# Second product accumulated onto the first, a quarter moved to GpSimd, the last rows in one transfer: attention and a mixture of experts on one core

## The chip, the core and the metric

The kernel runs on one core of a Trainium2 chip. The metric is the time of one execution on the device in microseconds; a number for a kernel is the median of its runs. The engines are TensorE (PE, with its weight loader PEld), VectorE (DVE), ScalarE (ACT), GpSimd (POOL) and SyncE (SP), which only issues transfers here. Transfers run on 16 DMA engines that the queues of SP and ACT share.

## The reference

Rotary attention over 2 batches x 8 heads x 576 positions x 64, then a dense mixture of 4 experts over the 1152 rows of 512 that come out of it.

```python
def rotate(x):
    x1, x2 = (x[..., :half], x[..., half:])
    return np.concatenate([x1 * cos - x2 * sin, x1 * sin + x2 * cos], axis=-1)
scores = scale * np.matmul(q_rot, k_rot.transpose(0, 1, 3, 2))
attn = softmax(scores)                      # over the keys, with 1e-9 in the divisor
x = np.matmul(attn, v)                      # as 1152 rows of 512
p = domain_probs / (domain_probs.sum(-1, keepdims=True) + 1e-09)
for e in range(4):
    h = np.maximum(x @ w1[e], 0.0)          # 512 -> 1024
    out += p[:, e:e + 1] * (h @ w2[e])      # 1024 -> 512
```

## The kernel before

All matrices of the experts are split into a high and a low part (`wh`, `wl`, `xH`, `xL`, `hH`, `hL`), and a product is three matmuls: high by high, high by low, low by high. `split` writes the high part on one engine (for weights ACT, L136) and the low part on another (for weights POOL, L143).

The rows go through the experts in two chunks: chunk 0 is 512 rows of batch 0, interleaved with the attention of batch 1; chunk 1 is the other 640 rows and starts at about 349 us, with nothing else running beside it. Its 640 rows end in `acc1_0` to `acc1_4`, of 128 rows each; `acc1_4` holds the last 64 rows of both batches, which lie 576 rows apart in the output.

Chunk 1 (`Moe1`) makes the first layer `x @ w1` with seven products of quarter size in place of eight (a Strassen-Winograd scheme). `TERMS` names for each of `p1` to `p7` a weight operand (a quarter of `w1` or a sum `s0` to `s3` of quarters) and a row operand (a quarter of `x`, or a sum `t1` to `t4`). The sums of weights are made by `Weights.sum`: four additions into `sf` (L538; on DVE, for the very first block on POOL), then `split` into `sh` (ACT) and `sl` (POOL). The sums of rows are made by `Quarters`: `whole` joins high and low (L666), `less` subtracts (L671), `high` and `low` split again (`tH`, L678 on ACT; `tL`, L682). They are issued in steps spread over the end of chunk 0; the last five steps come just before chunk 1, with the sums `s2`, `s3` of the second half on DVE.

A product is six matmuls of 128 x 320 (two j by three parts) into one of eight PSUM banks, which `bank` hands out in turn: four for `p1` of the four blocks of the first expert, four (`ahead`) for `p2`, then round. What follows a product is written in `product`: ACT copies `p1` to SBUF; DVE adds `p1` to `p6` (giving `u`), `u` to `p7` (`v`), and so on; `hidden` adds a remaining term in PSUM on DVE (L789), lets ACT write the high half of the hidden row through Relu (L797) and leaves the low half on DVE (L799) for after the next product. In the first expert the order is `p1` of the four blocks, `p2` of the four blocks, then `p6 p7 p5 p4 p3` per block; in the others `p1 p6 p7 p5 p2 p4 p3` per block.

The second layer (`second_layer`) is 8 x 5 x 3 matmuls of 128 x 512 into five banks `po`, each followed after its last matmul by `mix` on DVE (L633), which adds the weighted result to `acc`. In the last expert `mix` also stores: four times 128 rows from the SP queue (L639), and for `acc1_4` two halves of 64 rows, one from SP and one from ACT (L642).

`wts.next()` loads the next block of weights (SP) and splits an earlier one (ACT, POOL, and for `w1` DVE too). `second_layer` calls it four times per expert, `first_layer` after `p4` of each block. Every engine works in the order in which the program issues to it; waits are set by the framework from what reads and writes which tile.

Of the kernel before, what the change touches and what calls it, by code (L numbers as in the profile page):

```python
# [56 lines left out]
def kernel(  # L57
# [17 lines left out]
    nc = tc.nc  # L75
# [6 lines left out]
    SM = NR * P  # L82
# [398 lines left out]
    class Weights:  # L481
# [47 lines left out]
        def sum(self, raw, e, fb):  # L529

            a = raw.rearrange("p (j k h f) -> p j k h f", j=2, h=2, f=P)
            a11, a12, a21, a22 = (a[:, j, :, h, :] for h in range(2) for j in range(2))
            x = self.pool.tile([P, 4, 2, P], F32, tag="sf", name=f"sf{e}_{fb}", bufs=2)
            for o, p, q, op in (
                (0, a21, a22, ALU.add), (2, a11, a21, ALU.subtract), (1, x[:, 0], a11, ALU.subtract),
                (3, a12, x[:, 1], ALU.subtract),
            ):
                (nc.vector if e or fb else nc.gpsimd).tensor_tensor(out=x[:, o], in0=p, in1=q, op=op)  # L538
            sh, sl = (
                self.pool.tile([P, 4, 2, P], F32R, tag=f"s{t}", name=f"s{t}{e}_{fb}", bufs=NF // FB) for t in "hl"  # L540
            )
            split(nc.scalar, nc.gpsimd, x, sh, sl)
            self.sums[e, fb] = sh, sl

        def next(self):
# [3 lines left out]
    class Moe:  # L549
# [77 lines left out]
        def mix(self, e, t, po):  # L627
# [8 lines left out]
            if e == E - 1:  # L636
# [3 lines left out]
                else:  # L640
                    for b in range(B):
                        (nc.sync, nc.scalar)[b].dma_start(  # L642
                            out=out[b * S + SM : (b + 1) * S, :], in_=acc[b * ST : (b + 1) * ST]
                        )

    class Quarters:
# [46 lines left out]

        def second(self, eng, j):

# [6 lines left out]
            yield True  # L702
            self.whole(eng, "s3", j, 1, 0)
            self.less(eng, "s3", ("s3", "s2"))
            self.low(eng, "s0", 2, j)
# [15 lines left out]
    class Moe1(Moe):  # L721
# [7 lines left out]
        def __init__(self, ctx, quarters):  # L729
# [6 lines left out]
            ]  # L736
            self.used, self.ahead = 4, [self.bank(f"p2_{i}", i) for i in range(4)]
            self.x, self.lows = {}, []
# [9 lines left out]
        def product(self, e, i, p):  # L748
# [7 lines left out]
            (wh, wl), (xh, xl) = ws, self.quarters.operand(x)  # L756
            o = self.bank(f"{p}{e}_{i}")[:, 0:TH]
            for j in range(2):
                nc.tensor.matmul(o, lhsT=wh[:, j], rhs=xh[:, j], start=(j == 0), stop=False)  # L759
                nc.tensor.matmul(o, lhsT=wh[:, j], rhs=xl[:, j], start=False, stop=False)  # L760
                nc.tensor.matmul(o, lhsT=wl[:, j], rhs=xh[:, j], start=False, stop=(j == 1))  # L761
            x, lows = self.x, self.lows
            self.lows = []
            if p == "p1":
                x["p1", i] = self.temp("p1", e, i, NF // FB)
                nc.scalar.activation(out=x["p1", i], in_=o, func=AF.Copy)
# [9 lines left out]
            elif p == "p2":  # L776
                self.hidden(e, 2 * i, 0, o, x["p1", i])
            elif p == "p4":
# [11 lines left out]

        def hidden(self, e, f, t, o, other):

            if f not in self.hh:
                self.hh[f] = [self.h.tile([P, self.n], F32R, tag=f"h{x}{f}", name=f"h{x}1_{e}_{f}") for x in "HL"]
            hi, lo = (x[:, t * TH : (t + 1) * TH] for x in self.hh[f])
            self.add(o, o, other)
            nc.scalar.activation(out=hi, in_=o, func=AF.Relu)  # L797
# [6 lines left out]
        def first_layer(self, e):  # L804
# [3 lines left out]
            if e == 0:  # L808
                for i in range(nb):
                    self.product(e, i, "p1")  # L810
                wts.next()
                for i in range(nb):
# [4 lines left out]
            for i in range(nb):  # L817
                for p in ("p6", "p7", "p5", "p4", "p3") if e == 0 else ("p1", "p6", "p7", "p5", "p2", "p4", "p3"):
                    self.product(e, i, p)
                    if p == "p4" and e:  # L820
                        wts.next()
# [14 lines left out]
        def second_layer(self, e):  # L836
            n = self.n
            po = [self.bank(f"po1_{e}_{t}") for t in range(n // P)]
            for f in range(NF):
                fb, fi = divmod(f, FB)  # L840
                wH, wL = (w[:, fi, :] for w in wts.got[1, e, 1, fb])
                for t in range(n // P):
# [4 lines left out]
                    if f == NF - 1:  # L847
                        self.mix(e, t, po[t])
                if fi == FB - 1:
                    wts.next()  # L850
# [296 lines left out]
```

## Time and profile before

| what | us |
|---|---|
| runs (3): median, lowest, highest | 568.88, 568.68, 569.23 |
| the profiled execution | 566.62 |
| its span, first to last instruction | 564.8 |
| PE busy | 539.7 (96%) |
| POOL busy | 339.3 (60%) |
| DVE busy | 324.0 (57%) |
| ACT busy | 281.0 (50%) |

All views below are of the one profiled execution, and their times count from the first instruction. In a row of a timeline the first number is the start, the second the duration; in brackets stand the idle time of the engine before it and the instruction that ended it. A matmul's duration is longer than its step: they overlap in the array, so idle time is read from starts or from the brackets. The granted TensorE clock is 0.996 of full speed (2.4 GHz) over the span, and 1.00 wherever PE works from 349 us on.

### The profile page before, as it was taken

To read this page: it belongs to the slowest core of one execution; us is meant where nothing else is said; L and a number is where in the kernel's file an instruction comes from. 1 tells how busy PE (TensorE), PEld (TensorE's weight loads), DVE (VectorE), ACT (ScalarE), POOL (GpSimd) and SP (SyncE) were. 2 spreads that over 40 slices of the span, in tenths; PEclk is the share of its full clock that TensorE was granted. 3 is DMA by queue.
4 is the path that set the end of the run, shared out by engine and by line. 5 is a ranking of instruction groups with operands and counts; after the bars stand their busy time and mean duration, and the time that the engine had idled before them with its cause. 6 is when DMAs were issued, how large, how long until landed. Compare 5 with 4: busy or idle time off the path is not lost. (4 is left out here: it accounts for less than half of the span.)

```text
span 564.8 us, 8507 instructions
## 1 busy us (share of the span) xinstructions
PE 539.7 (96%) x3157; PEld 474.3 (84%) x3157; DVE 324.0 (57%) x587; ACT 281.0 (50%) x561; POOL 339.3 (60%) x240
## 2 busy tenths in 40 slices
PE   4898998999999999999999999999999999999996
PEld 3787887788888888888888888888898899889985
DVE  5588897244363534453344546994587668757702
ACT  5688888555444545555545553453344234324400
POOL 7999984558715871487433487458554655565400
PEclk9899999999999999999999999999999999999999
DMA  5245023352234123432142214522223213222102
GB/s 153 71 117 145 17 51 99 81 173 93 77 113 140 41 76 102 131 97 64 62 128 74 62 52 150 185 76 74 77 77 111 74 39 113 78 76 85 61 1 93
DMA packets 48732, 50.68 MB, mean 90 GB/s; under 512 B 15538, under 2 KB 38322, under 8 KB 48690
## 3 DMA queue, kind: packets, MB, share of 16 engines
q1 hardware_dynamic: 47890, 49.38, 29.0%
q10 hardware_dynamic: 800, 0.75, 0.5%
q8 instruction: 25, 0.41, 0.3%
q14 instruction: 17, 0.14, 0.1%
HBM read 43.34 MB, written 2.36 MB: 81 GB/s over the span
## 5 line engine op out<-in xcount | busy, mean ns | idle before, releaser
L143 POOL TENSOR_TENSOR wl<-wr,wh 128x1024 fp32r<-128x1024 f32 x64 | 154.4, 2413 | 136.0 <-ACT wh L136 136.0
L136 ACT ACTIVATE wh<-wr 128x1024 fp32r<-128x1024 f32 x64 | 67.2, 1052 | 26.5 <-PE po L600 11.9
L300 DVE TENSOR_REDUCE mx<-sc 128x1 f32<-128x576 f32 x72 | 54.2, 753 | 37.7 <-PE sc L289 37.0
L143 POOL TENSOR_TENSOR sl<-sf,sh 128x1024 fp32r<-128x1024 f32 x16 | 38.5, 2407 | 43.0 <-ACT sh L136 43.0
L846 PE MATMUL po<-wh,hL 128*128 128x512 f32 x160 | 62.3, 389 | 0.0
L845 PE MATMUL po<-wl,hH 128*128 128x512 f32 x160 | 62.3, 389 | 0.0
L844 PE MATMUL po<-wh,hH 128*128 128x512 f32 x160 | 62.3, 389 | 0.0
L308 ACT ACTIVATE e<-sc,mx 128x576 f32<-128x576 f32 x72 | 53.3, 740 | 17.7 <-DVE mx L300 16.7
L584 DVE SCALAR_TENSOR_TENSOR hL<-ph,hH 128x512 fp32r<-128x512 f32 x32 | 22.1, 692 | 60.1 <-ACT hH L583 60.1
L598 PE MATMUL po<-wh,hH 128*128 128x512 f32 x128 | 52.3, 409 | 0.0
L136 ACT ACTIVATE sh<-sf 128x1024 fp32r<-128x1024 f32 x16 | 17.0, 1060 | 70.5 <-DVE sf L538 64.9
L623 PE MATMUL ph<-xH,wh 128*128 128x512 f32 x128 | 51.5, 402 | 0.0
L624 PE MATMUL ph<-xL,wh 128*128 128x512 f32 x128 | 50.1, 392 | 0.4 <-POOL xL L424 0.4
L343 DVE TENSOR_TENSOR ptL<-pp,ptH 128x512 fp32r<-128x512 f32 x64 | 44.0, 687 | 11.1 <-ACT ptH L339 10.3
L339 ACT ACTIVATE ptH<-pp 128x512 fp32r<-128x512 f32 x64 | 38.1, 595 | 24.6 <-PE x L372 17.3
L600 PE MATMUL po<-wh,hL 128*128 128x512 f32 x128 | 50.3, 393 | 0.0
L625 PE MATMUL ph<-xH,wl 128*128 128x512 f32 x128 | 50.1, 392 | 0.0
L599 PE MATMUL po<-wl,hH 128*128 128x512 f32 x128 | 50.0, 391 | 0.0
L797 ACT ACTIVATE hH<-p 128x320 fp32r<-128x320 f32 x64 | 27.1, 436 | 40.3 <-DVE p L789 40.3
L322 PE MATMUL pp<-ident,e 128*128 128x128 f32 x288 | 44.7, 279 | 2.1 <-DVE ptL L343 1.1
L538 DVE TENSOR_TENSOR sf<-wr 128x256 f32<-128x256 f32 x30 | 32.7, 1129 | 16.9 <-DMA wr<-in_moe_w_dram 16.9
L322 PEld LDWEIGHTS pp<-ident,e 128*128 128x128 f32 x288 | 34.2, 142 | 8.1 <-ACT e L308 2.4
(171 smaller groups left out, 1373.4 us busy)
## 6 DMA issues: line engine op xcount, KB each, us to landing
wr<-in_moe_w_dram SPq DMA_DIRECT2D x68, 512.0 KB, 3.6
k2T<-kT SPq DMA_DIRECT2D x14, 288.0 KB, 4.1
rawv<-in_v_dram SPq DMA_DIRECT2D x16, 128.0 KB, 3.0
out_dram<-acc SPq DMA_DIRECT2D x8, 256.0 KB, 4.0
rawk<-in_k_dram SPq DMA_DIRECT2D x7, 256.0 KB, 3.8
rawq<-in_q_dram SPq DMA_DIRECT2D x7, 256.0 KB, 3.1
rawv<-in_v_dram SPq DMA_DIRECT2D x16, 32.0 KB, 2.3
tabs<-in_rope_dram ACTq DMA_DIRECT2D x1, 320.0 KB, 3.4
```

Of the source, the lines that this page charges most:

```text
L136: nc.scalar.activation(out=hi, in_=src, func=AF.Copy)
L143: eng_l.tensor_tensor(out=lo, in0=src, in1=f32(hi), op=ALU.subtract)
L300: nc.vector.tensor_reduce(out=mx, in_=self.sc[u][:, :, 0:HALF], op=ALU.max, axis=AX.XY, negate=True)
L308: nc.scalar.activation(out=e.rearrange("p (i c) -> p i c", i=2), in_=self.sc.pop(u)[:, :, 0:HALF], func=AF.Exp, bias=self.mx.pop(u), accum ...
L322: nc.tensor.transpose(pp[:, c * P : (c + 1) * P], self.e[u][:, c * P : (c + 1) * P], ident)
L598: nc.tensor.matmul(po[t], lhsT=sH, rhs=wH, start=(f == 0), stop=False)
L600: nc.tensor.matmul(po[t], lhsT=sL, rhs=wH, start=False, stop=(f == NF - 1))
L623: nc.tensor.matmul(o, lhsT=wH[:, kt], rhs=xh, start=(kt == 0), stop=False)
L624: nc.tensor.matmul(o, lhsT=wH[:, kt], rhs=xl, start=False, stop=False)
L844: nc.tensor.matmul(po[t], lhsT=sH, rhs=wH, start=(f == 0), stop=False)
L845: nc.tensor.matmul(po[t], lhsT=sH, rhs=wL, start=False, stop=False)
L846: nc.tensor.matmul(po[t], lhsT=sL, rhs=wH, start=False, stop=(f == NF - 1))
```

## The change

- `p2` no longer gets a bank and an addition of its own: its six matmuls go on accumulating in the bank of `p1` of the same block, after ACT has copied `p1` out. `hidden` then has no DVE addition for it. The four banks `ahead` go to the first `p6`, `p7`, `p5`, `p4`.
- In `Quarters.second`, the sum `s3` (one `whole`, one `less`) of the second half goes from DVE to POOL.
- The split of the first weight sums (`sh0_0` on ACT, `sl0_0` on POOL) is issued after the second `p1` product instead of with its sum.
- In experts 1 to 3 the last `wts.next()` of the expert before is issued after the first `p1` instead of at the end of `second_layer`.
- The last 128 rows are stored by one transfer from the ACT queue, its destination written as 2 x 64 x 512, instead of two of 64 rows.

```diff
@@ Weights.sum
-            split(nc.scalar, nc.gpsimd, x, sh, sl)
             self.sums[e, fb] = sh, sl
+            if e or fb:
+                split(nc.scalar, nc.gpsimd, x, sh, sl)
+            else:
+                self.first_sums = lambda: split(nc.scalar, nc.gpsimd, x, sh, sl)
@@ Moe.mix
-                    for b in range(B):
-                        (nc.sync, nc.scalar)[b].dma_start(
-                            out=out[b * S + SM : (b + 1) * S, :], in_=acc[b * ST : (b + 1) * ST]
-                        )
+                    nc.scalar.dma_start(out=out.rearrange("(b s) d -> b s d", s=S)[:, SM:S, :], in_=acc)
@@ Quarters.second
-        def second(self, eng, j):
+        def second(self, eng, j, other=nc.gpsimd):
...
-            self.whole(eng, "s3", j, 1, 0)
-            self.less(eng, "s3", ("s3", "s2"))
+            self.whole(other, "s3", j, 1, 0)
+            self.less(other, "s3", ("s3", "s2"))
@@ Moe1.product
-            o = self.bank(f"{p}{e}_{i}")[:, 0:TH]
+            onto = p == "p2"
+            o = self.x.pop(("p1 sum", i)) if onto else self.bank(f"{p}{e}_{i}")[:, 0:TH]
...
-                nc.tensor.matmul(o, lhsT=wh[:, j], rhs=xh[:, j], start=(j == 0), stop=False)
+                nc.tensor.matmul(o, lhsT=wh[:, j], rhs=xh[:, j], start=(j == 0 and not onto), stop=False, **group)
...
             if p == "p1":
+                x["p1 sum", i] = o
...
             elif p == "p2":
-                self.hidden(e, 2 * i, 0, o, x["p1", i])
+                self.hidden(e, 2 * i, 0, o)
@@ Moe1.hidden
-            self.add(o, o, other)
+            if other is not None:
+                self.add(o, o, other)
@@ Moe1.first_layer
                     self.product(e, i, "p1")
+                    if i == 1:
+                        wts.first_sums()
...
-                    if p == "p4" and e:
+                    if e and (p == "p4" or i == 0 and p == "p1"):
                         wts.next()
@@ Moe1.second_layer
-                if fi == FB - 1:
+                if fi == FB - 1 and f < NF - 1:
                     wts.next()
```

At the start of chunk 1, ACT's instructions stand so before. `tH<-s01`, `s21`, `s31` are the high parts of the last row sums, `p1_0_i<-p10_i` the copy of `p1` of block i out of its bank `p10_i`, `sh0_i` the high part of the weight sums of block i.

```order
L136 ACTIVATE sh0_0_3972<-sf0_0_3967 128x1024
L678 ACTIVATE tH_3707<-s01_3872 128x320
L678 ACTIVATE tH_3707<-s21_3936 128x320
L678 ACTIVATE tH_3707<-s31_3986 128x320
L766 ACTIVATE p1_0_0_4017<-p10_0_4010 128x320
L766 ACTIVATE p1_0_1_4026<-p10_1_4019 128x320
L766 ACTIVATE p1_0_2_4035<-p10_2_4028 128x320
L766 ACTIVATE p1_0_3_4044<-p10_3_4037 128x320
L136 ACTIVATE sh0_1_4053<-sf0_1_4048 128x1024
L797 ACTIVATE hH1_0_0_4063<-p2_0_4006 128x320
```

And so after it, on the same engine:

```order
L678 ACTIVATE tH_3707<-s01_3872 128x320
L678 ACTIVATE tH_3707<-s21_3936 128x320
L678 ACTIVATE tH_3707<-s31_3984 128x320
L769 ACTIVATE p1_0_0_4015<-p10_0_4008 128x320
L769 ACTIVATE p1_0_1_4024<-p10_1_4017 128x320
L136 ACTIVATE sh0_0_3972<-sf0_0_3967 128x1024
L769 ACTIVATE p1_0_2_4035<-p10_2_4028 128x320
L769 ACTIVATE p1_0_3_4044<-p10_3_4037 128x320
L136 ACTIVATE sh0_1_4053<-sf0_1_4048 128x1024
L801 ACTIVATE hH1_0_0_4063<-p10_0_4008 128x320
```

`sh0_0` moved from ahead of the three `tH` to between the second and third copy, and the first hidden half now reads the bank of `p1`.

POOL at the same place before: the sums `sf0_0` of the first block, then the low parts `sl0_i` of the weight sums.

```order
L538 TENSOR_TENSOR sf0_0_3967<-wr1_0_2_0_3894 128x256 x2
L538 TENSOR_TENSOR sf0_0_3967<-sf0_0_3967,wr1_0_2_0_3894 128x256
L538 TENSOR_TENSOR sf0_0_3967<-wr1_0_2_0_3894,sf0_0_3967 128x256
L143 TENSOR_TENSOR sl0_0_3973<-sf0_0_3967,sh0_0_3972 128x1024
L143 TENSOR_TENSOR sl0_1_4054<-sf0_1_4048,sh0_1_4053 128x1024
```

And after:

```order
L538 TENSOR_TENSOR sf0_0_3967<-wr1_0_2_0_3894 128x256 x2
L538 TENSOR_TENSOR sf0_0_3967<-sf0_0_3967,wr1_0_2_0_3894 128x256
L538 TENSOR_TENSOR sf0_0_3967<-wr1_0_2_0_3894,sf0_0_3967 128x256
L666 TENSOR_TENSOR s31_3984<-xH1_74,xL1_76 128x320
L671 TENSOR_TENSOR s31_3984<-s31_3984,s21_3936 128x320
L143 TENSOR_TENSOR sl0_0_3973<-sf0_0_3967,sh0_0_3972 128x1024
L143 TENSOR_TENSOR sl0_1_4054<-sf0_1_4048,sh0_1_4053 128x1024
```

The two operations of `s3` stand on POOL between the first sums and their low part.

DVE after the change, from the first expert's last operations for chunk 0 on (`tL` low parts of row sums, `hL1_0_f` low hidden halves; the additions `p2_i<-p2_i,p1_0_i` that stood among the `hL` before are gone, and so are the two operations of `s3` ahead of the `tL`):

```order
L636 SCALAR_TENSOR_TENSOR acc0_3_1520<-po0_3_3_3685,probs_78,acc0_3_1520 128x512
L682 TENSOR_TENSOR tL_3708<-s01_3872,tH_3707 128x320
L682 TENSOR_TENSOR tL_3708<-s21_3936,tH_3707 128x320
L682 TENSOR_TENSOR tL_3708<-s31_3984,tH_3707 128x320
L538 TENSOR_TENSOR sf0_1_4048<-wr1_0_2_1_3927 128x256 x2
L538 TENSOR_TENSOR sf0_1_4048<-sf0_1_4048,wr1_0_2_1_3927 128x256
L538 TENSOR_TENSOR sf0_1_4048<-wr1_0_2_1_3927,sf0_1_4048 128x256
L803 SCALAR_TENSOR_TENSOR hL1_0_0_4064<-p10_0_4008,hH1_0_0_4063 128x320
L803 SCALAR_TENSOR_TENSOR hL1_0_2_4073<-p10_1_4017,hH1_0_2_4072 128x320
L803 SCALAR_TENSOR_TENSOR hL1_0_4_4083<-p10_2_4028,hH1_0_4_4082 128x320
L538 TENSOR_TENSOR sf0_2_4098<-wr1_0_2_2_3961 128x256 x2
```

The weight sums `sf0_1` follow directly on the `tL`, and three low halves in a row on them.

## Rows read from the trace of the kernel before

**Rows 1.** Busy us by window: PE, PEld, DVE, ACT, POOL, then clock, DMA share, GB/s.
```profile
349.00:371.00 22.00, 20.09 (x129) 18.60 (x128) 20.78 (x44) 9.65 (x18) 10.34 (x7) 1.00 0.52 178
371.00:560.00 189.00, 188.95 (x1026) 169.79 (x1025) 119.42 (x224) 66.06 (x109) 97.99 (x41) 1.00 0.22 72
560.00:564.80 4.80, 0.00 (x0) 0.00 (x0) 0.74 (x2) 0.00 (x0) 0.00 (x0) 0.93 0.59 190
```

**Rows 2.** Waits of PEld, 348 to 564.8: who for whom, us in total, times, longest.
```profile
PEld p L759 <- DVE hL L799: 2.0, 3, 1.0
PEld p L759 <- ACT p L766: 0.6, 1, 0.6
PEld p L761 <- POOL sl L143: 0.5, 1, 0.5
PEld p L759 <- DVE acc L633: 0.4, 1, 0.4
```

**Rows 3.** Timeline of PE and PEld: first `p2`, first `p6`, a wait.
```profile
352.43 0.31 PE L759 MATMUL p<-xH,wh 128*128 128x320 f32 x1
...
356.83 0.19 PEld L759 LDWEIGHTS p<-tH,sh 128*128 128x128 f32 x1 [0.60 <-ACT p L766]
...
364.38 0.19 PEld L759 LDWEIGHTS p<-t1H,sh 128*128 128x128 f32 x1 [0.75 <-DVE hL L799]
```

**Rows 4.** Tail: timeline; transfers with KB, us to landing; packets, MB, engines' share by queue.
```profile
560.77 0.55 ACTq L642 DMA_DIRECT2D out_dram<-acc  x1
...
out_dram<-acc SPq DMA_DIRECT2D x1, 128.0 KB, 3.0
...
out_dram<-acc SPq DMA_DIRECT2D x3, 256.0 KB, 2.5
...
q10 hardware_dynamic: 80, 0.13, 15.6%
```

**Rows 5.** Timeline of ACT: `sh0_0`, the third `tH`, the four copies of `p1`.
```profile
351.41 1.06 ACT L136 ACTIVATE sh<-sf 128x1024 fp32r<-128x1024 f32 x1 [5.56 <-POOL sf L538]
...
355.84 0.47 ACT L678 ACTIVATE tH<-s 128x320 fp32r<-128x320 f32 x1 [2.65 <-DVE s L671]
356.34 1.43 ACT L766 ACTIVATE p<-p 128x320 f32<-128x320 f32 x4
```

**Rows 6.** POOL: the form of L666 (ns min/median/max); timeline of `sl0_0`, `sl0_1`.
```profile
L666 POOL TENSOR_TENSOR s<-xH,xL x6: 862/875/884, 322.4 to 340.8; 128x320 f32<-128x320 f32 x6
...
352.54 2.39 POOL L143 TENSOR_TENSOR sl<-sf,sh 128x1024 fp32r<-128x1024 f32 x1 [1.17 <-ACT sh L136]
359.71 2.40 POOL L143 TENSOR_TENSOR sl<-sf,sh 128x1024 fp32r<-128x1024 f32 x1 [4.77 <-ACT sh L136]
```

**Rows 7.** Timeline of DVE: `s3`, the `tL`, end of `sf0_1`, `sf0_2`, `hL1_0_6`.
```profile
353.45 1.83 DVE L666 TENSOR_TENSOR s<-xH,xL 128x320 f32<-128x320 f32 x1
...
355.73 1.29 DVE L682 TENSOR_TENSOR tL<-s,tH 128x320 fp32r<-128x320 f32 x3
...
358.05 0.42 DVE L538 TENSOR_TENSOR sf<-wr,sf 128x256 f32<-128x256 f32 x1
...
361.99 0.75 DVE L538 TENSOR_TENSOR sf<-wr 128x256 f32<-128x256 f32 x2
...
363.85 0.48 DVE L799 SCALAR_TENSOR_TENSOR hL<-p,hH 128x320 fp32r<-128x320 f32 x1
```

**Rows 8.** The additions of `p1` to `p2`: count, ns min/median/max, first and last start.
```profile
L789 DVE TENSOR_TENSOR p<-p,p x16: 489/491/492, 358.4 to 531.7; 128x320 f32<-128x320 f32 x16
```

**Rows 9.** DMA packets in 20.3:20.8 (`probs`, 128 plain rows) and 21.0:22.0 (2 x 64).
```profile
DMA packets 144, 0.01 MB, mean 17 GB/s; under 512 B 144, under 2 KB 144, under 8 KB 144
...
DMA packets 130, 0.00 MB, mean 2 GB/s; under 512 B 130, under 2 KB 130, under 8 KB 130
```

**Rows 10.** Busy time by stretch, columns as rows 1: the stores at the tail.
```profile
562.00:562.50 0.50, 0.00 (x0) 0.00 (x0) 0.00 (x0) 0.00 (x0) 0.00 (x0) 1.00 0.89 184
...
562.70:562.85 0.15, 0.00 (x0) 0.00 (x0) 0.00 (x0) 0.00 (x0) 0.00 (x0) 1.00 1.04 383
```

## What I predict, and why

> **What bounds the kernel now.** I read first the table of engine busy time by stretch: in the 189 us from 371 to 560 TensorE (PE) idles 0.05 us in sum, in the 22 us from 349 to 371 it idles 1.9 us, and after 560 it does nothing for 4.8 us [rows 1]. So from 371 to 560 only fewer or faster matmuls would help, and the change takes none away and makes none faster. It can act at two places only: the start of the second chunk (349 to 371) and the tail. Next I read what PE's weight loader waited for from 348 on: 3.5 us in six waits, for VectorE's (DVE) low halves, ScalarE's (ACT) copy of a product, GpSimd's (POOL) low weight sums and the last sums of chunk 0 [rows 2]. The order of time shows where they lie: the second products start at 352.43; the first `p6` comes at 356.83, after 0.60 us for the `p1` copy; a wait of 0.75 for a low half ends at 364.38 [rows 3], and the longest, 1.0 [rows 2], is the last, just before 370. At the tail the last accumulator's two halves are issued at 560.77 on the ACT and SP queues; the later one lands 3.0 us after that [rows 4], at 563.8, and the span ends at 564.8, 1.0 us behind. The profiled execution took 566.62 us, 2.26 below the median of 568.88; I make the sum as a difference to its span and add it to the median.
>
> **Start of chunk 1: what is late now.** Three edits meet here. (a) `p2` goes onto `p1`'s bank, so its first matmul must wait until ACT has copied `p1`. (b) The last quarter `s3` (two operations) goes from DVE to POOL. (c) The first sums' split (`sh0_0` on ACT, `sl0_0` on POOL) is put behind the first two copies. In the order after, ACT's chain is three `tH`, copies 0 and 1, `sh0_0`, copies 2 and 3; the third `tH` waits for POOL's `s3`.
> POOL has the sum `sf0_0` ready at 351.37, just before the 351.41 at which ACT starts `sh0_0` now [rows 5]. Two operations at 0.875 us each, POOL's own price in six rows of this form [rows 6], end `s3` at 353.12. (DVE needed 1.83 us for the first of them alone, as POOL held it up [rows 7].) From the start of this `tH` to the matmul that needs the copy took 0.99 us before (355.84 to 356.83) [rows 3, 5]. So `p2` starts at 354.15 instead of 352.43: PE loses 1.7 us which it does not lose now. Against that fall the 0.4 us wait on the sums of chunk 0 and the 0.60 us wait of `p6` [rows 2, 3]. The 24 matmuls of the four `p2` took 4.40 us from 352.43 to 356.83, less these two waits 3.4, 0.143 each; they put `p6` at 357.6, 0.8 us later than now.
> ACT reaches `sh0_0` at 353.16 + 0.50 + 2 x 0.36 = 354.4 and ends it at 355.45 [rows 5]; POOL's `sl0_0` takes 2.39 us [rows 6], 355.5 to 357.9. `p6`'s third matmul wants it at 357.9: just in time.
> **Where the stall goes.** DVE loses two operations and four adds here, but it is then held by POOL. A DVE operation that reads two SBUF tiles does not get on while POOL runs a long one: `s` L666, begun at 353.45, took 1.83 us and ended 0.35 us after POOL's `sl0_0` (352.54 + 2.39) [rows 6, 7]; the pair of `sf0_2` begun at 361.99 got going as `sl0_1` ended at 362.11 [rows 6, 7]. After the change DVE is through with chunk 0 at 353.5, with three `tL` (1.29 us [rows 7]) at 354.8, and the four operations of `sf0_1` would run from 354.7 to 356.2; but `sl0_0` begins at 355.5. The third is under way by then; the fourth waits until 357.9 and ends at 358.3, against 358.47 now [rows 7]. Then `sh0_1`, `sl0_1` and `sf0_2` follow as before, 0.17 us earlier. The four removed adds of 0.49 us [rows 8] stood between 358.4 and 362, while DVE's `sf0_2` could not start anyway. The low half `hL1_0_6`, for whose bank PE waits at 364, ends at 364.16 instead of 364.33 [rows 7], so PE goes on at 364.2 instead of 364.38 [rows 3], and the chain from there to 370 is the same work. Sum of this place: **-0.2 us**. Bounds: -3.5 us if every wait of rows 2 vanished, +1.7 us if the new wait came on top of all that is there; I take -0.2, since it comes from the rows one by one.
>
> **Experts 1 to 3.** Twelve more adds go, and one weight step per expert (its load, DVE's sum, two ACT and two POOL splits) comes behind the first `p1`. Nothing stands between its old and new place on SP, DVE or POOL; on ACT the copy of `p1` now comes ahead of the two splits. `p2` waits for a copy made three products earlier. PE idles 0.05 us here [rows 1], so the cost is nothing either way; what covers it is PE's own queue, and without that cover a late copy would cost its 0.36 us [rows 5]. Accumulating costs PE nothing extra: five of six matmuls of each product already do it, at the 0.143 us above.
>
> **The tail.** One transfer of 256 KB on the ACT queue takes the place of two of 128 KB. Its source has 128 rows, but its destination is written as 2 x 64 x 512. The trace has one transfer of that form, the last load of `probs` (2 x 64 rows in DRAM, 128 in SBUF). Every transfer ends with one small closing packet per DMA engine: the half store on queue q10 makes 80 packets, 64 rows and 16 closings [rows 4]; a `probs` load of 128 plain rows makes 144, 128 and 16; the 2 x 64 load makes 130, 128 and **2** [rows 9]. So that form runs on 2 of the 16 engines, 64 rows each. I carry this over to the store.
> The price: with all 16 engines busy they move 383 GB/s, 23.9 per engine; during the first half of the old store, 184 GB/s at a share of 0.89, 12.9 per busy engine [rows 10]. 128 KB per engine take 5.5 us at the one and 10.2 us at the other. I take the first: an engine alone on its queue has the least to share, and it is the pace of the other half, of rows of the same kind. A 256 KB store on 16 engines needs 0.7 us of this and lands 2.5 us after issue [rows 4], so 1.8 us are fixed; the new one lands 7.3 us after issue instead of 3.0. Nothing covers it: PE, DVE and POOL are done. **+4.3 us** (between -0.5, landing as a plain 256 KB store does, and +9.0).
> The Trainium skill says the same as the packet count (DMA: Bandwidth & Descriptors, Why a DMA increments its semaphore by 16 and not by 1): a transfer uses the largest number of engines, up to 16, that divides the slowest dimension of both patterns. Of 2 and 128 that is 2, so by it the sum stays as it is, and the rule speaks against this edit; the trace agrees with 2 closing packets.
>
> Sum: -0.2 + 0 + 4.3 = +4.1 us: 570.7 for a profiled execution, 573.0 for the median.
>
> **Rivals.** *The store spreads over 16 engines* after all, because what holds for a load need not for a store. It then lands 2.5 us after issue, the tail gives 0.5, and with the start's -0.2 the time is 568.2, no slower than before. The deciding point is 16 closing packets against 2. For it: no store of this form is in the trace. Against it: a transfer has both patterns whichever way it goes. Chance 0.09. The Trainium skill has a fit (same page, Anatomy of one DMA — SWDGE (gpsimd) path: 2.0 us plus bytes at 436 GB/s, for another issuing path than this) by which 256 KB would take an estimated 2.6 us, as in this rival; no run here shows that path.
> *Two engines at the slow pace* of 12.9 GB/s: +9.0 - 0.2, 577.7. For it: the ACT queue's half ran so. Against: 16 engines then read half the partitions at once, two do not. Chance 0.10, half of it at paces in between.
> *DVE gets through before POOL*: if `sf0_1` is ready before `sl0_0` starts (it is 0.7 us short), the waits at 364 and 370 fall and PE gains 1 to 3.5 us at the start: 569.7 to 572.2 with the tail. Chance 0.12.
> *The start gets dearer*: the third operation of `sf0_1` is held too, or the 1.7 us wait comes on top: 573.4 to 574.9. It lies inside the range; I count it with the forecast.
>
> **How the numbers follow.** Forecast 573.0, chance 0.69. The range reaches down to 571.2 (half of the start's possible gain) and up to 576.0 (a pace of 15.6 GB/s: 8.4 us instead of 5.5), and leaves out the spread store, the slowest pace and the full gain, some 2 in 10. Within 0.2%, about what a measurement here can tell, is 567.7 to 570.0: the spread store and the tip of the third rival, 0.10. Faster needs both at once, 0.03. Slower 0.87.
>
> **What would show it.** Right: from the last DVE operation to the end 8 us instead of 4, with the DMA share near 0.12 (2 of 16) and 2 closing packets; PE idles 1.7 us before the second products, with ACT's `p1` copy named as releaser, and still waits for `hL` near 364 and 370; no wait in experts 1 to 3. Wrong: a tail of 4 us or less; PE's waits from 349 to 371 summing to under 2.5 us or over 5; any new wait after 371.

## The result, and the profile after

The changed kernel takes 573.50 us (median of 6 runs, 571.61 to 574.08) against 568.84 (6 runs, 568.10 to 569.23): a ratio of 1.0079, 95% interval 1.0063 to 1.0095, 4.7 us more. Its profiled execution took 574.03 us, its span is 572.2, so it stands 0.5 above its median, while the one of before stood 2.2 below its own.

Because of that the two traces can't be compared end to end. I cut each at two marks. *S* is the end of the attention's last operation on DVE, the low half of its last output rows (L424); these rows belong to chunk 1 (the expectations below call them chunk 0's). All the work ahead of S is the same in every kernel here, yet S lies between 347.9 and 350.8 us over the fourteen profiles, and 1.5 us apart in two profiles of one and the same kernel. *T* is the issue of the last store. From S to T is the **stretch** that the edits at the start of chunk 1 and in the experts can move; from T to the end of the span is the **tail**.

S and T in the traces, before and then after (the T of before is in [rows 4]); timeline of DVE and of ACT's queue, start, duration:

```profile
346.55 1.38 DVE L424 TENSOR_TENSOR xL<-xf,xH 128x512 fp32r<-128x512 f32 x1
```

```profile
348.64 1.38 DVE L424 TENSOR_TENSOR xL<-xf,xH 128x512 fp32r<-128x512 f32 x1
...
562.69 1.12 ACTq L644 DMA_DIRECT2D out_dram<-acc  x1
```

| us | before | after | difference |
|---|---|---|---|
| S | 347.93 | 350.02 | +2.1 (from execution to execution) |
| stretch, S to T | 212.84 | 212.67 | -0.17 |
| tail, T to the end of the span | 4.03 | 9.51 | +5.48 |

So the start of chunk 1 and the experts together gained 0.2 us and the last store lost 5.5. (Spans are given to 0.1 us, so a tail is good to 0.05.)

Waits of PE's weight loader in the changed kernel from 348 us on, in the form of [rows 2]; below them the busy time by stretch, in the columns of [rows 1]:

```profile
PEld p L761 <- ACT p L769: 1.8, 1, 1.8
PEld p L761 <- DVE hL L803: 1.3, 2, 1.0
```

```profile
349.00:371.00 22.00, 20.38 (x130) 19.17 (x128) 19.92 (x36) 8.55 (x18) 13.46 (x10) 1.00 0.58 191
371.00:560.00 189.00, 188.25 (x1025) 169.73 (x1026) 114.73 (x213) 66.59 (x110) 98.66 (x41) 1.00 0.23 70
```

Of the six waits of [rows 2] three are left. The one for the `p1` copy has grown from 0.6 to 1.8 us and stands ahead of the second products instead of ahead of `p6`; those for POOL's `sl` and for `acc` are gone; of the three for low halves two stayed. The 0.75 us that PE idles after 371 is the end of the last of these, which reaches to 371.75 here because this execution runs 2.1 us late; it is no new wait.

The start of chunk 1, timelines of PEld, ACT, POOL and DVE, one after the other:

```profile
356.27 0.19 PEld L761 LDWEIGHTS p<-xH,wh 128*128 128x128 f32 x1 [1.85 <-ACT p L769]
...
359.75 0.19 PEld L761 LDWEIGHTS p<-tH,sh 128*128 128x128 f32 x1
...
366.30 0.19 PEld L761 LDWEIGHTS p<-t1H,sh 128*128 128x128 f32 x1 [0.27 <-DVE hL L803]
...
371.75 0.19 PEld L761 LDWEIGHTS p<-t1H,sh 128*128 128x128 f32 x1 [1.04 <-DVE hL L803]
```

```profile
355.29 0.47 ACT L678 ACTIVATE tH<-s 128x320 fp32r<-128x320 f32 x1 [1.92 <-POOL s L671]
355.78 0.77 ACT L769 ACTIVATE p<-p 128x320 f32<-128x320 f32 x2
```

```profile
354.39 0.87 POOL L671 TENSOR_TENSOR s<-s,s 128x320 f32<-128x320 f32 x1
357.57 2.53 POOL L143 TENSOR_TENSOR sl<-sf,sh 128x1024 fp32r<-128x1024 f32 x1 [2.31 <-ACT sh L136]
```

```profile
357.41 0.42 DVE L538 TENSOR_TENSOR sf<-sf,wr 128x256 f32<-128x256 f32 x1
357.87 2.52 DVE L538 TENSOR_TENSOR sf<-wr,sf 128x256 f32<-128x256 f32 x1
```

In order of time: POOL ends `s3` at 355.26, the third `tH` on ACT follows at 355.29, the copies of `p1` at 355.78, and PE goes on at 356.27. On DVE the third operation of `sf0_1` was under way when POOL began `sl0_0` at 357.57, and took its 0.42 us; the fourth, of the same size, came 0.3 us after POOL's start and took 2.52.

The tail after, the columns of [rows 1] (the last two are the share of the 16 DMA engines and GB/s), and the packets of the ACT queue, in the form of the last row of [rows 4]:

```profile
562.50:563.50 1.00, 0.00 (x0) 0.00 (x0) 0.15 (x1) 0.00 (x0) 0.00 (x0) 1.00 1.05 346
563.50:564.50 1.00, 0.00 (x0) 0.00 (x0) 0.00 (x0) 0.00 (x0) 0.00 (x0) 1.00 0.28 86
564.50:565.50 1.00, 0.00 (x0) 0.00 (x0) 0.00 (x0) 0.00 (x0) 0.00 (x0) 1.00 0.15 33
565.50:566.50 1.00, 0.00 (x0) 0.00 (x0) 0.00 (x0) 0.00 (x0) 0.00 (x0) 0.51 0.09 25
566.50:567.50 1.00, 0.00 (x0) 0.00 (x0) 0.00 (x0) 0.00 (x0) 0.00 (x0) 0.50 0.13 49
567.50:568.50 1.00, 0.00 (x0) 0.00 (x0) 0.00 (x0) 0.00 (x0) 0.00 (x0) 0.50 0.13 51
```

```profile
q10 hardware_dynamic: 130, 0.26, 6.2%
```

In the first of these rows the other stores still run, at 346 GB/s; the last of their packets end at 563.95. Then only the last store is left: a share of 0.13 is 2 of 16 engines, at 25 GB/s each, and before it reaches that pace there are two microseconds at 33 and 25 GB/s for both together. 130 packets are 128 rows and 2 closings.

### The profile page after: what moved, and what is told of

The parts are those of the page before. It is cut to its first block, busy times and chain, and to the rows that moved or that the text cites. A ratio compares the mean times of both kernels' runs of the same rounds, so it can differ in the third digit from the quotient of the medians.

```text
span 572.2 us, 8485 instructions
## 1 busy us (share of the span) xinstructions
PE 541.3 (95%) x3157; PEld 475.6 (83%) x3157; DVE 320.3 (56%) x569; ACT 280.5 (49%) x561; POOL 340.8 (60%) x242
```

## The experiments

Twelve runs, on three chips, each beside runs of the kernel before. `tail_back` and the seven runs from `own_bank` on hold the two half stores of before, so that their tail is out of the way and the stretch shows the start alone; the other four vary the last store. Medians stand where a kernel was timed. Each ratio is to the runs of before that were made beside it (median 568.71 of 17 for `tail_back` and `tail_only`, 568.16 of 23 for the last two) and is not the quotient of the two medians.

| run | stretch | tail | median (runs), ratio to before |
|---|---|---|---|
| before | 212.84 | 4.03 | 568.84 (6) |
| after | 212.67 | 9.51 | 573.50 (6), 1.0079 [1.0063, 1.0095] |
| tail_back | 212.65 | 4.08 | 567.92 (12), 0.9995 [0.9982, 1.0009] |
| tail_only | 212.83 | 9.58 | 572.79 (6), 1.0086 [1.0066, 1.0106] |
| tail_two_queues | 212.66 | 9.90 | |
| tail_plain_rows | 212.65 | 3.50 | |
| tail_half_cols | 212.64 | 6.45 | |
| own_bank | 212.62 | 4.03 | |
| s3_dve | 214.08 | 4.08 | |
| s3_dve_warm | 212.72 | 4.09 | |
| low_first | 212.48 | 3.86 | |
| sums_first | 211.40 | 4.06 | |
| sums_first_timed | 211.39 | 4.00 | 567.43 (12), 0.9983 [0.9967, 0.9998] |
| s3_early | 214.63 | 4.03 | 570.11 (12), 1.0034 [1.0018, 1.0050] |

The stretch repeats well: five kernels that differ in the store alone have it within 0.03 us (212.64 to 212.67), and two profiles of one kernel within 0.01. Differences of 0.1 us in it are read as real.

### Which half of the change costs

`tail_back` is the changed kernel with the two half stores, `tail_only` the kernel before with the one transfer.

```diff
-                    nc.scalar.dma_start(out=out.rearrange("(b s) d -> b s d", s=S)[:, SM:S, :], in_=acc)
+                    for b in range(B):
+                        (nc.sync, nc.scalar)[b].dma_start(
+                            out=out[b * S + SM : (b + 1) * S, :], in_=acc[b * ST : (b + 1) * ST]
+                        )
```

> The changed kernel with the last rows stored by two halves again (64 rows from SP, 64 from ACT); all else as changed. Theory (the one transfer of 2 x 64 rows runs on 2 DMA engines and is the whole loss; the start of chunk 1 gains 0.2 us): from the issue of the last store to the end of the span 4.1 us as before instead of 9.5, from the end of VectorE's last low half of chunk 0 (line 424) to that issue 212.7 us as changed, median 568.6 us. Rival (something else in the change costs the 4.7 us, such as the new wait of the second product or the moved weight step): that stretch stays longer than before by some us and the median stays above 571.

> The kernel before with nothing changed but the last store: one transfer of 2 x 64 rows from the ACT queue. Theory: 9.5 us from the issue to the end of the span (9 to 10), 64 packets of 2 KB on each of 2 engines, 2 closing packets, median 573.7 us, slower than the whole change by the 0.2 us that the start gains. Rival (the loss needs the other edits): the tail stays at 4 to 5 us, median 569 to 570.

Measured: without the transfer the rest of the change makes no difference that can be told (0.9995, interval from 0.9982 to 1.0009; stretch 212.65, tail 4.08). The transfer alone makes 1.0086, tail 9.58. The whole loss is the store. Of the other four edits the accumulation and the move of `s3` are taken back one by one below; the later split of the first sums and the moved weight step were not run alone.

### What the store's price is made of

Two queues: the same 2 x 64 form, the left half of the columns from SP and the right half from ACT.

```diff
-                    nc.scalar.dma_start(out=out.rearrange("(b s) d -> b s d", s=S)[:, SM:S, :], in_=acc)
+                    ends = out.rearrange("(b s) d -> b s d", s=S)[:, SM:S, :]
+                    for eng, (x, y) in ((nc.sync, (0, DM // 2)), (nc.scalar, (DM // 2, DM))):
+                        eng.dma_start(out=ends[:, :, x:y], in_=acc[:, x:y])
```

> The changed kernel, the last 2 x 64 rows stored by two transfers of half the columns, one on the SP queue and one on the ACT queue, each still written as 2 x 64. Theory (what counts is the pair of DMA engines that a 2 x 64 pattern gets, the same pair on either queue): still about 9.5 us from issue to the end, 9 to 10, 4 closing packets. Rival (one transfer on one queue is the limit, so a second queue halves it): about 6.8 us.

Plain rows: `acc1_4` goes to 128 rows with one step between them, those of the fourth accumulator.

```diff
-                if t < NR:
+                if self.c and t == 3:
+                    pass
+                elif t < NR:
...
-                    nc.scalar.dma_start(out=out.rearrange("(b s) d -> b s d", s=S)[:, SM:S, :], in_=acc)
+                    rows = out[self.c * S : self.c * S + SM, :].rearrange("(p r) d -> p r d", r=NR)
+                    nc.scalar.dma_start(out=rows[:, 3, :], in_=acc)
```

> The changed kernel, but the last accumulator is stored as one transfer of 256 KB from the ACT queue to 128 evenly spaced rows (those of the fourth accumulator, whose own store is left out; the last 64 rows of both batches are left out too). Theory (the pattern's first size 2 is the cause, not the size of the transfer, the queue or the single issue): 16 closing packets and 3.3 to 4.1 us from issue to the end. Rival (one transfer of 256 KB from ACT is slow as such): about 9.5 us.

Half the columns:

```diff
-                    nc.scalar.dma_start(out=out.rearrange("(b s) d -> b s d", s=S)[:, SM:S, :], in_=acc)
+                    ends = out.rearrange("(b s) d -> b s d", s=S)[:, SM:S, :]
+                    nc.scalar.dma_start(out=ends[:, :, 0 : DM // 2], in_=acc[:, 0 : DM // 2])
```

> The changed kernel with the last store in the 2 x 64 form on the ACT queue, but of the first 256 of 512 columns alone: 64 packets of 1 KB on each of two engines instead of 2 KB. Left out: the other half of these columns of the last 64 rows of both batches. Theory (the two engines are bound by bytes, with a slow beginning): the data take 3.4 to 3.7 us instead of 6.7, and from the issue to the end of the span 6.1 to 6.5 us pass instead of 9.5. Rival (a packet costs its 80 to 105 ns whatever its size): 9.5.

Measured: a second queue doesn't help (9.90 instead of 9.51), since it brings no other engines: each of its two transfers closes with 2 packets, and with both under way the share stays at 2 of 16, as this row shows:

```profile
566.50:567.50 1.00, 0.00 (x0) 0.00 (x0) 0.00 (x0) 0.00 (x0) 0.00 (x0) 0.50 0.12 31
```

Plain rows of the same 256 KB end 3.50 us after issue. Half the bytes end 6.45 us after issue. In these two kernels the packets of the ACT queue are, plain rows first, then half the columns:

```profile
q10 hardware_dynamic: 144, 0.26, 5.0%
```

```profile
q10 hardware_dynamic: 130, 0.13, 3.2%
```

128 rows and 16 closings against 128 rows and 2: source, queue and size of the plain rows are those of the changed kernel; the form of the destination differs, and one store of 256 KB fewer runs ahead of it. So the number of engines that carry the store makes the loss. The Trainium skill states it as a rule (DMA: Bandwidth & Descriptors, Why a DMA increments its semaphore by 16 and not by 1: the largest number of engines up to 16 that divides the sizes of the slowest dimension on both sides); the trace agrees, with 2 engines for 2 x 64 and 16 for 128.

The busy time by stretch of the kernel with half the columns, columns as before:

```profile
565.50:566.50 1.00, 0.00 (x0) 0.00 (x0) 0.00 (x0) 0.00 (x0) 0.00 (x0) 0.99 0.12 37
566.50:567.50 1.00, 0.00 (x0) 0.00 (x0) 0.00 (x0) 0.00 (x0) 0.00 (x0) 0.50 0.12 42
```

So the engines are bound by bytes: in the packet records of the two traces a row of 2 KB takes 84 ns (median) in the changed kernel, one of 1 KB 46 ns here. 64 rows on each engine come to 5.4 us and 2.9 us; the data took 6.7 us and 3.6. The difference is a few packets that stall: in the changed kernel ten of the first 32, those of the first 2.3 us, took between 198 and 529 ns, and of the 96 behind them one took over 160; in `tail_only` ten stall again, nine at the same places and one a packet later, up to 564 ns. What they wait for is open; nothing was tried on it.

### Is it the accumulation, or the place of the wait

`own_bank` takes the accumulation back: `p2` in a bank of its own, the 16 additions on DVE again.

```diff
-            onto = p == "p2"
-            o = self.x.pop(("p1 sum", i)) if onto else self.bank(f"{p}{e}_{i}")[:, 0:TH]
-            group = dict(skip_group_check=True) if p in ("p1", "p2") else {}
+            onto = False
+            o = self.bank(f"{p}{e}_{i}")[:, 0:TH]
+            group = {}
...
-                self.hidden(e, 2 * i, 0, o)
+                self.hidden(e, 2 * i, 0, o, x["p1", i])
```

> The changed kernel with the two half stores back, and p2 again in a bank of its own with the VectorE addition behind it; the banks ahead as before; all else as after. The same stretch as above. Theory: TensorE does not wait for the p1 copy before p2, but waits about as long (1.4 to 1.5 us) before or in the first p6 for GpSimd's sl0_0, which the later s3 and split hold back; the 16 additions on VectorE hide: 212.7, within 0.2 of after. Rival one (the additions taken off VectorE are what keeps after level with before): 214.3, with longer waits for low halves. Rival two (the wait of p2 is a cost of its own): 211.0.

Measured: 212.62, within 0.05 of the changed kernel. The waits of PE's weight loader:

```profile
PEld p L766 <- POOL sl L143: 1.5, 1, 1.5
PEld p L764 <- DVE hL L806: 1.3, 2, 1.1
PEld p L764 <- DVE acc L636: 0.4, 1, 0.4
```

The 1.8 us before `p2` are gone and 1.5 us for `sl0_0` and 0.4 for `acc` stand in their place. So the accumulation, the first edit of the change, is worth nothing here in either direction: sixteen additions of 490 ns leave DVE, which PE does not wait for at that point, and the new wait only comes earlier than one that PE had to sit out.

### Moving s3 back: right mechanism, wrong time

```diff
-        def second(self, eng, j, other=nc.gpsimd):
+        def second(self, eng, j, other=None):
+            other = other or eng
```

> The changed kernel with the two half stores back, and in it the last quarter s3 back on VectorE; the first weight sums still split behind the second copy. The measure is the stretch from the end of chunk 0's last operation on VectorE's row sums to the issue of the last store: 212.84 us before, 212.66 after. Theory (a VectorE operation that reads two SBUF tiles is held while a long GpSimd operation runs): s3 on VectorE, with GpSimd idle, ends about 1.2 us later than on GpSimd, so TensorE waits about 2.9 us for the p1 copy instead of 1.8; but the fourth operation of sf0_1 now ends near 357.0, just before GpSimd's sl0_0 begins, the serial sums come earlier against TensorE, and the waits for low halves at 366 and 371 vanish: 212.2 to 212.3 us, 0.4 less than after. Rival (a later p2 just adds its delay): about 213.9.

Measured: 214.08, the rival's 213.9 rather than 212.3. But the waits say the theory's mechanism happened: one wait is left, 3.1 us for the `p1` copy, and none for a low half, where the rival would have kept them. What neither had is in PE's timeline and in the granted clock (the column behind the busy times):

```profile
354.79 0.31 PE L768 MATMUL p<-xH,wl 128*128 128x320 f32 x1
357.98 0.57 PE L766 MATMUL p<-xH,wh 128*128 128x320 f32 x1 [2.88 <-ACT p L774]
358.34 0.47 PE L767 MATMUL p<-xL,wh 128*128 128x320 f32 x1
358.61 0.47 PE L768 MATMUL p<-xH,wl 128*128 128x320 f32 x1
```

```profile
354.90:357.90 3.00, 0.20 (x2) 0.00 (x0) 2.96 (x7) 0.89 (x3) 0.00 (x0) 1.00 0.89 237
357.98:359.50 1.52, 1.52 (x6) 1.52 (x7) 1.49 (x5) 1.52 (x4) 0.23 (x1) 0.53 1.05 402
359.50:361.20 1.70, 1.70 (x8) 1.70 (x7) 0.17 (x2) 1.62 (x4) 1.70 (x1) 0.50 0.74 184
...
362.00:371.00 9.00, 9.00 (x63) 9.00 (x63) 8.28 (x19) 3.21 (x6) 4.64 (x2) 1.00 0.25 91
```

After 2.88 us without work PE comes back and the granted clock falls to 0.50, the 1.2 GHz level: until 361.3 its matmuls start 0.27 us apart instead of 0.147. By the starts the first thirteen steps of `p2` take 3.55 us, and 2.01 in the changed kernel: 1.5 us. After the 1.6 us that PE idles at the same place in the changed kernel (its weight loader 1.85) the clock stays at 1.00 (2.4 GHz). To tell this from a delay on the other engines, `s3_dve_warm` fills the wait with matmuls that nobody reads:

```diff
+                wh = wts.got[1, e, 0, 0][0][:, 0:2, 0:P]
+                xh = self.quarters.operand("x00")[0]
+                for i in range(20):
+                    nc.tensor.matmul(self.ahead[3][:, 0:TH], lhsT=wh[:, 0], rhs=xh[:, 0], start=True, stop=True)
                 for i in range(nb):
                     self.product(e, i, "p2")
```

> The kernel with s3 back on VectorE (two half stores), and in the 3.1 us in which TensorE waits there for the p1 copy, 20 matmuls of 128 x 320 more, whose product nobody reads (20 x 0.143 = 2.9 us at full clock). Theory (the 1.8 us by which that kernel missed 212.3 are the lower granted clock that follows the idle time: 13 matmuls of p2 stepped 0.27 us instead of 0.143): with TensorE kept busy the clock stays at full speed, the second products start at the same place and step 0.143, and the stretch from the end of chunk 0's last row operation on VectorE to the last store's issue is 212.3 to 212.5 us. Rival (the later p2 itself costs the 1.8, through the serial chain on the other engines): it stays at 214.1, or gets longer by the added work.

Measured: 212.72. The second products start at the same distance from S as without the filling (7.54 us), at full clock and full pace:

```profile
354.41 1.48 PE L826 MATMUL p<-xH,wh 128*128 128x320 f32 x9
355.83 0.42 PE L766 MATMUL p<-xH,wh 128*128 128x320 f32 x1
356.08 0.31 PE L767 MATMUL p<-xL,wh 128*128 128x320 f32 x1
356.23 0.31 PE L768 MATMUL p<-xH,wl 128*128 128x320 f32 x1
```

```profile
355.83:359.00 3.17, 3.17 (x22) 3.17 (x22) 1.61 (x5) 3.17 (x7) 1.87 (x1) 1.00 0.92 330
```

1.36 us came back by giving PE useless work, of the 1.43 by which `s3_dve` stood above `tail_back`: the lower clock was its cost. My 212.3 for `s3_dve` was too low even at full clock: by the starts in the traces the later `p2` costs 1.29 us against the changed kernel and the waits for low halves that fall give 1.3, so nothing is gained, and 212.7 is what this kernel has.

### The order of the serial work on DVE and POOL

`low_first`: the weight sums of blocks 2 and 3 are issued behind the `p6` of blocks 0 and 1, so that no low half queues behind a sum that POOL holds up.

```diff
-                wts.split()
...
+                    if e == 0 and i < 2 and p == "p6":
+                        wts.split()
...
-                    wts.split()
+                    if i:
+                        wts.split()
```

> The changed kernel with the two half stores back; in the first expert the weight sums of blocks 2 and 3 are issued behind the p6 of blocks 0 and 1, so that on VectorE the u and the last low half come ahead of sf0_2 and no low half waits behind a sum that GpSimd holds up. Theory (the waits near 366 and 371 come from this order, and the chain sums, high part, low part of a block takes 1.5 + 1.06 + 2.4 = 5.0 us against TensorE's 4.3 per block): the waits for hL vanish, TensorE waits about 1 us for the low part of a later block instead; the stretch is 212.0 us, 0.7 less than after. Rival (the low halves alone are the wait): both waits go for good, 211.3. Rival (order does not matter, TensorE is held elsewhere): 212.7.

Measured: 212.48, the waits as expected in kind:

```profile
PEld p L764 <- ACT p L772: 1.8, 1, 1.8
PEld p L766 <- POOL sl L143: 0.9, 1, 0.9
PEld p L764 <- DVE hL L806: 0.2, 1, 0.2
```

Of 1.3 us for low halves 0.2 is left, and 0.9 us for the low part of a later block has come. I had expected a gain of 0.7 us; it is 0.2. I read this as the chain of sums, high part and low part being the limit there, whichever of its links PE meets; the next run tests it.

`sums_first` attacks that chain by two edits together: `sf0_1` is made ahead of the three `tL`, and its split follows on that of the first sums.

```diff
...
+        quarter_step()
+        wts.split()
-        for _ in range(5):
+        for _ in range(4):
             quarter_step()
...
                     if i == 1:
-                        wts.first_sums()
-                wts.next()
+                        wts.first_sums[0]()
+                wts.load()
+                wts.first_sums[1]()
```

> The changed kernel with the two half stores back; the sum sf0_1 is made ahead of the last three low parts of the row sums (tL), and its split is issued behind that of the first sums, so that GpSimd has two long operations back to back. Theory (VectorE's operations on two SBUF tiles do not start until a long GpSimd operation ends, and two back to back leave no gap): the tL of s21 and s31 end only after the second one, TensorE waits about 2 us for them at the first p7, the stretch is 213.1 us. Rival (VectorE gets in between two GpSimd operations, or runs beside them): 211.5 to 212.0.

> The kernel with the sum sf0_1 ahead of the last three tL and two half stores, timed. Its stretch from the end of chunk 0's last row operation to the last store was 1.4 us shorter than before's, and its tail is as before's: 567.3 us, ratio 0.9975. Rival (the gain of one trace is chance): no change, 568.7.

Measured: 211.40 and, in a second profile, 211.39. My theory said 213.1, and it fell; the rival said 211.5 to 212.0. PE's only wait is the 1.8 us for the copy. Timed, the kernel stands at 0.9983 of before, interval 0.9967 to 0.9998: at the edge of what a measurement can tell, but on the right side of before. The rows of DVE and POOL (first profile) show where the theory was wrong:

```profile
357.03 3.10 DVE L685 TENSOR_TENSOR tL<-s,tH 128x320 fp32r<-128x320 f32 x2
357.18 2.60 POOL L143 TENSOR_TENSOR sl<-sf,sh 128x1024 fp32r<-128x1024 f32 x1 [2.31 <-ACT sh L136]
...
357.43 2.70 DVE L685 TENSOR_TENSOR tL<-s,tH 128x320 fp32r<-128x320 f32 x1
...
357.18 5.22 POOL L143 TENSOR_TENSOR sl<-sf,sh 128x1024 fp32r<-128x1024 f32 x2 [2.31 <-ACT sh L136]
...
360.05 1.27 DVE L806 SCALAR_TENSOR_TENSOR hL<-p,hH 128x320 fp32r<-128x320 f32 x3
```

The first two `tL` were through or under way when POOL began at 357.18. The third was held, but only to the end of the first of POOL's two operations: it ended at 360.13, and POOL's pair took 5.22 us instead of two times 2.40, 0.2 us more on each of the two. A waiting operation of DVE passes at the end of the POOL operation that held it; it is not starved by a second one queued there. Nor is every operation of DVE held: the three low halves from 360.05 on, which read one operand from PSUM and one from SBUF, took 1.27 us together while POOL's second operation ran.

`s3_early` is `sums_first` with one edit more and tries to shorten the wait that is left: `s3` on POOL ahead of the last of the four operations of `sf0_0`.

```diff
                 (nc.vector if e or fb else nc.gpsimd).tensor_tensor(out=x[:, o], in0=p, in1=q, op=op)
+                if o == 1 and not e and not fb:
+                    quarters[0].third(nc.gpsimd, 1)
...
```

> As the one before, with s3's two operations on GpSimd ahead of the last of the four operations of the sum sf0_0 instead of behind it. TensorE's wait for the p1 copy, the only one left, should fall from 1.8 to 0.9 us, since the third tH waits for s3. Theory: the stretch falls from 211.4 to 210.5 us, and the median is 566.4, ratio 0.996. Rival (the fourth operation of sf0_1, due to start within 0.1 us of GpSimd's sl0_0, is held up by it for 2.5 us): the sums of the next block and the three tL come later, TensorE waits about 0.9 us at the first p7, and nothing is gained: 211.4.

Measured: 214.63, ratio 1.0034 (1.0018 to 1.0050): slower than before, and neither theory nor rival. The wait for the copy did fall, to 1.2 us. But:

```profile
357.01 2.70 DVE L687 TENSOR_TENSOR tL<-s,tH 128x320 fp32r<-128x320 f32 x1
356.90 5.01 POOL L143 TENSOR_TENSOR sl<-sf,sh 128x1024 fp32r<-128x1024 f32 x2 [1.63 <-ACT sh L136]
...
357.01 5.25 DVE L687 TENSOR_TENSOR tL<-s,tH 128x320 fp32r<-128x320 f32 x2
359.32 2.59 POOL L143 TENSOR_TENSOR sl<-sf,sh 128x1024 fp32r<-128x1024 f32 x1
```

```profile
PEld p L771 <- DVE tL L687: 2.6, 1, 2.6
...
362.31 0.63 PE L771 MATMUL p<-tL,sh 128*128 128x320 f32 x1 [2.34 <-DVE tL L687]
```

```profile
362.30:365.40 3.10, 3.09 (x11) 3.09 (x12) 3.07 (x9) 0.05 (x1) 0.00 (x0) 0.50 0.21 82
```

POOL began 0.11 us ahead of the first `tL` (356.90 to 357.01). The first `tL` passed at the end of the first POOL operation (359.71), the second at the end of the second (362.26), and PE stood 2.6 us for it and came back at half clock for another 3.1 us. In `sums_first` the order of the two was the other way round, with the first `tL` 0.56 us ahead (at 356.62). Held operations pass one by one, so it matters how many are left when a long POOL operation begins.

## Why the prediction was right, and where it was off

**The start of chunk 1, -0.2 us: measured -0.17.** It came true row by row. PE was to lose 1.7 us ahead of `p2`, which it does not lose before: measured from S, `p2` starts 1.75 us later. `p6` was to come 0.8 us later: 0.83 (PEld takes its first weights at 359.75 after and 356.83 before). PE was to go on 0.17 us earlier after the wait for the low half near 364: 0.17, at 366.30 after and 364.38 before, both counted from S. The waits for `sl` and `acc` were to fall, and fell. The third operation of `sf0_1` was to be under way and the fourth held until POOL is done: 0.42 and 2.52 us in the rows above. The waits for low halves were to stay: two of the three did, with 1.04 us as the longest. `tail_back`, at 0.9995 of before, says the same of the whole. One of the two rows that I gave for the hold does not show it: the pair of `sf0_2` begun at 361.99 took 0.75 us in all, as the pair of `sf0_1` at 356.93 did with POOL idle; the 1.83 us of `s` does show it, and so do the runs above. That POOL holds DVE up is also what the Trainium skill states (SBUF — State Buffer, Who interferes with whom: a VectorE instruction with two inputs in SBUF contends with a GpSimd instruction that reads SBUF; their shared pair of ports is an exclusive lock, and issue order decides who blocks); the trace agrees, with 0.42 us become 2.52.

**Experts 1 to 3, nothing: measured nothing.** No wait of PE begins after 371 except the end of the one at 371.75.

**The tail, +4.3 us: measured +5.5.** The form was right: 2 engines, 2 closing packets, a share of 0.13. This is the one term that was mis-sized. I had 5.5 us of data at 23.9 GB/s per engine; the pace when nothing stalls is 24.4 (2 KB in 84 ns), but the data took 6.7 us, because packets in the first 2.3 us stall. I had kept that case as a rival of its own, the slow pace of 12.9 GB/s per engine for the whole transfer [rows 10]. For two microseconds the average came near it: 33 and 25 GB/s on two engines are 16.5 and 12.5 each; then the pace I took set in. The kind was another: in the half store of before a row on the ACT queue took 160 ns (median of the packet records), while here most took 84 from the start and ten stalled. The 1.2 us more of data are the whole of the error, since the parts around them, 1.3 us from issue to the first packet and 1.5 us from the closing packet to the end, make the 2.8 us that I carried over (1.8 to landing and 1.0 behind it).

**The sum.** In the traces the change costs 5.3 us (-0.17 + 5.48), in the medians 4.7 (interval 3.6 to 5.4); `tail_only` costs 4.1 in the medians of its runs (interval 3.8 to 6.0 by its ratio). The forecast of 573.0 against 573.50 is closer than its largest term was, and that closeness is luck: the tail was 1.2 us off in the traces, and the medians happen to show some 0.6 us less of it.

**The rivals.** The store did not spread over 16 engines. DVE did not get through before POOL; it was short by the 0.7 us that I gave (without POOL its fourth operation would have ended at 358.29, and POOL began at 357.57). What the rival would have been worth is shown by `sums_first`, whose sums are through in time: 1.3 us of stretch, inside the 1 to 3.5 that I gave. The start did not get dearer; `s3_dve` and `s3_early` show that it could have, by 1.4 and 2.0 us, in part through a cause that no rival held, the clock (in `s3_early` beside the held `tL`).

## What to carry to other kernels

Before two transfers are joined into one, count the closing packets of a transfer of that form in the trace: they tell how many DMA engines it will use, and a saved issue is worth nothing when 2 engines carry what 16 did. Taking work off an engine that PE does not wait for (sixteen additions here) gives back nothing; follow the wait that an edit ends to what is late next. Where DVE and POOL share a serial stretch, look at which of the two starts first, since 0.7 us there, between `sums_first` and `s3_early`, moved the end by three, the fall of the clock included.

## What the runs showed of the hardware

- An idle PE can cost twice. After 2.88 us (`s3_dve`) and 2.34 us (`s3_early`) without work the granted clock was 0.50 for some 3 us and matmuls stepped 0.27 us; after 1.6 us in the changed kernel and in `sums_first` it stayed 1.00. Useless matmuls in the wait of `s3_dve` gave 1.36 us back.
- A DVE operation of 128 x 320 that reads two SBUF tiles and is held by a POOL operation ends some 0.35 us after it, whether or not another POOL operation is queued (360.13 after 359.78; 359.71 after 359.36; 362.26 after 361.91): one operation passes at each POOL boundary.
- A transfer on two engines ran at 24.4 GB/s per engine for rows of 2 KB and 22 for rows of 1 KB, with ten packets of 198 to 564 ns in its first 2.3 us in two profiles of the 2 KB form; a second queue added nothing.
- One and the same work up to S ended between 347.9 and 350.8 us in fourteen profiles; the stretch after it repeated within 0.03.
